# Tokens per expert counted once for all batches, and the last output columns stored in two halves

## The chip, the cores and the metric

The kernel runs on one core of a Trainium2 chip. The metric is the device time of one execution in microseconds (us), given as the median of the runs. TensorE (PE) does the matrix products, VectorE (DVE) and ScalarE (ACT) the elementwise work and the evictions from PSUM, GpSimd (POOL) some subtractions and the weight loads, and SyncE (SP) issues most of the other DMAs.

## The reference

Packed attention, and a mixture of experts behind it, for 8 batches of 576 tokens, 8 heads of 64:

```python
p_packed = sm_attn(p, k, v)                 # 32 packed rows for each head
out = sm_attn(q, p_packed, p_packed)        # back to 576 tokens
x = out.transpose(0, 2, 1, 3).reshape(4608, 512)
expert_idx = argmax(normalised(x) @ normalised(expert_emb).T / tau)
out[mask_e] = gate_w * (relu(x[mask_e] @ w1[e]) @ w2[e])   # e: the token's expert, of 8
```

## The kernel before

Each batch is tiled into five blocks of up to 128 tokens (`NC5`), and its feed-forward part runs with one expert, guessed early by `guess`. `route` computes the router's logits of all tokens and `oh`, a one-hot row of the chosen expert for each token; `counts` adds up `oh` over the tokens with two TensorE products against a column of ones, and `gates_main` multiplies the counts by `sel`, the one-hot row of the guessed expert, into `rest_f`. At the end of the program five VectorE operations turn `rest_f` into `rest_i`, the tokens that the guess did not cover; every engine loads their sum into a register and branches on it. A general path inside that branch does the uncovered batches anew; with these inputs it is passed over.

The order of work is written out by hand inside `tc.manual_schedule()`: engines run their instructions in the order in which the Python generators emit them. `ffn(b)` is the main stream. For each batch it emits `hidden` (the product with w1, 16 pieces f of 6 products each, line 932, evicted by ScalarE at 934 and VectorE at 935), then the columns of the last 320 tokens (line 960), then two blocks of 128 tokens, c = 0 and c = 1 (line 978). After each few products it yields, and the loop over `work` emits a step of the next batch's attention, `att_main(b + 1)`, with `route` at its end. While c = 1 runs, `ffn` also emits `w1_rows` of the next batch (line 850; the rows that go through w1). For the first batch the interleaving follows the string table `PLAN`.

`route` works in two groups of token blocks. For each block and half m, VectorE reduces the logits (line 704), and ScalarE squares the rows into a scratch tile `scr` only for their sum (line 708: an ACTIVATE and a read of the accumulator). `scr` has two buffers, taken in turn. PSUM tiles with the tag `pf` have four buffers, shared by `hidden`, the stored blocks and `counts`.

`store_main` gives the functions that store. A block is evicted by ScalarE (line 1254) and goes out as four DMAs of 32 token rows of 512 columns, 64 KB each (line 1264). In the last batch, block c = 1 is computed in two halves of 256 columns; both are evicted separately, and the four DMAs are issued after the second one, two by SyncE and two by ScalarE.

Of the kernel before, what the change touches and what calls it, by code (L numbers as in the profile page):

```python
# [17 lines left out]
P = 128  # L18
# [5 lines left out]
def kernel(  # L24
# [55 lines left out]
    for e in range(E):  # L80
        nc.vector.memset(ecol[:, e : e + 1], float(e))
    rest_f = cp.tile([1, B], F32, name="rest_f")
    rest_i = cp.tile([1, B + 1], I32, name="rest_i")

    def rsqrt(x, y, tag, eng=nc.vector):
# [66 lines left out]
    class Batch:  # L152
        def __init__(self):
            for name in ("kT", "qT", "s1", "mx", "p1", "sums", "rinv", "pp2", "s2", "p1T"):
                setattr(self, name, {})
            self.begun = self.soft = False

    def load_nat(b, n):

# [364 lines left out]
    def guess(x, late=0, engine=mybir.EngineType.Pool, total=None):  # L524
        pt = ps.tile([P, 512], F32, name="pu", tag="pf")
        if total is not None:

            for n in range(NPR):
                nc.tensor.matmul(
                    pt[:1, :E], total[:, n : n + 1], enT[:, n], start=(n == 0), stop=(n == NPR - 1)  # L530
                )
        else:
            for g in range(NG):
                nc.tensor.matmul(pt[:1, :E], itau, x.ppf[:, g, D:], start=(g == 0), stop=(g == NG - 1))
        yield
        m8 = sm.tile([1, 8], F32, name="m8", tag="m8")
        idx = sm.tile([1, 8], U32, name="idx", tag="idx")
        nc.vector.max(m8, pt[:1, :E])
        nc.vector.max_index(idx, m8, pt[:1, :E])
        gi = sm.tile([1, 1], F32, name="gi", tag="gi")  # L540
        nc.vector.tensor_copy(gi, idx[:, 0:1])
        x.sel = sm.tile([1, E], F32, name="sel", tag="sel")
        nc.vector.tensor_scalar(
            out=x.sel, in0=ecol[:1], scalar1=gi, scalar2=None, op0=ALU.is_equal
        )
        yield from idle(late)
        x.e = nc.values_load(idx[0:1, 0:1], engines=[engine], min_val=0, max_val=E - 1)
# [133 lines left out]
    def route(x, fine=False):  # L681
        lgs, sss = x.routed
        for c0, c1 in ((0, 2), (2, NC5)):
            pts = [pb.tile([P, 1024], F32, name="pt", tag="pb") for _ in range(2)]
            for c in range(c0, c1):
                for g in range(NG):
                    for n in range(2 * c, min(2 * c + 2, S // 64)):
                        for h in range(HB):
                            at = 512 * (h % 2) + 256 * g + XW * (c - c0)
                            nc.tensor.matmul(  # L690
                                pts[h // 2][64 * (n % 2) : 64 * (n % 2) + 64, at : at + XW],
                                x.at[32 * h : 32 * h + 32, g, 64 * n : 64 * n + 64],
                                x.ppf[32 * h : 32 * h + 32, g],
                                start=True,
                                stop=True,
                                tile_position=(32 * h, 64 * (n % 2)),
                            )
            yield
            views = [pt.rearrange("p (b s) -> p b s", s=256) for pt in pts]
            for c in range(c0, c1):  # L700
                r = rows(c)
                for m in range(2):
                    v = views[m][:r, :, XW * (c - c0) : XW * (c - c0) + XW]
                    nc.vector.tensor_reduce(  # L704
                        lgs[:r, m, c], v[:, :, D:].rearrange("p b e -> p e b"), axis=AX.X, op=ALU.add
                    )
                    scr = sb.tile([P, 4, D], F32, name="scr", tag="scr", bufs=2)
                    nc.scalar.activation(  # L708
                        scr[:r], v[:, :, :D], AF.Square, accum_out=sss[:r, m, c : c + 1]
                    )  # L710
                yield

        lg = sm.tile([P, NC5, E], F32, name="lgt", tag="lgt")
        ss = sm.tile([P, NC5], F32, name="sst", tag="sst")
        nc.vector.tensor_tensor(out=lg, in0=lgs[:, 0], in1=lgs[:, 1], op=ALU.add)
        nc.gpsimd.tensor_tensor(out=ss, in0=sss[:, 0], in1=sss[:, 1], op=ALU.add)
        x.lg, x.ss = lg, ss
        if fine:
            yield
        nc.vector.tensor_scalar_mul(lg, lg, itau)  # L720
        mx = sm.tile([P, NC5, 1], F32, name="lmx", tag="lmx")
        nc.vector.tensor_reduce(mx, lg, axis=AX.X, op=ALU.max)
        nc.vector.tensor_tensor(
            out=lg, in0=lg, in1=mx.broadcast_to([P, NC5, E]), op=ALU.subtract
        )
        oh = sm.tile([P, NC5, E], F32, name="oh", tag="oh")
        nc.vector.scalar_tensor_tensor(
            out=oh, in0=lg, scalar=0.0, in1=code.broadcast_to([P, NC5, E]),
            op0=ALU.is_ge, op1=ALU.mult,
        )  # L730
        nc.vector.tensor_reduce(mx, oh, axis=AX.X, op=ALU.max)
        nc.vector.tensor_tensor(
            out=oh, in0=code.broadcast_to([P, NC5, E]), in1=mx.broadcast_to([P, NC5, E]),
            op=ALU.is_equal,
        )
        x.oh = oh

    def counts(x):
        oh = x.oh
        pt = ps.tile([P, 512], F32, name="pu", tag="pf")  # L740
        nc.tensor.matmul(
            pt[:1, : 4 * E], ones, oh[:, 0:4].rearrange("p c e -> p (c e)"), start=True, stop=True
        )
        nc.tensor.matmul(pt[:1, 4 * E : 5 * E], ones[:64], oh[:64, 4], start=True, stop=True)
        cnt = sm.tile([1, E], F32, name="cnt", tag="cnt")
        nc.vector.tensor_reduce(
            cnt, pt[:1, : 5 * E].rearrange("p (c e) -> p e c", c=NC5), axis=AX.X, op=ALU.add
        )
        x.cnt = cnt


    def gates(x, eng=nc.vector):
# [115 lines left out]
                yield  # L868


    def ffn(x, store, late=False, after=None, end=False):
        if late:
            x.G = sb.tile([P, 2, NG, F], F32R, name="G", tag="G")
            x.g32, x.gs = [], 0
# [96 lines left out]
        for c in range(NCT):  # L971

            w = 256 if end and c == NCT - 1 else 512
            for at in range(0, 512, w):
                pf = ps.tile([P, 512], F32, name="pf", tag="pf")
                for f in range(NF):
# [17 lines left out]
                    if c == NCT - 1 and hasattr(after, "w1g"):  # L994
                        next(after.w1g, None)
                        next(after.w1g, None)
                    elif c == NCT - 1 and hasattr(after, "lg"):
                        after.w1g = w1_rows(after)
                        next(after.w1g)
                last.append((c, pf, at, w))  # L1000
# [2 lines left out]
            store(*t)  # L1003
        if hasattr(after, "w1g"):
            drain(after.w1g)

    STF = 5

# [9 lines left out]


    bat = [Batch() for _ in range(B)]  # L1020
    NAT = 2 * NPR + NG
    seq = [(b, i) for b in range(1, B) for i in range(NAT)]
    seq[NPR : 2 * NPR + NG] = [(1, i) for i in (8, 9, 4, 5, 6, 7)]
# [20 lines left out]
    def att_main(b):  # L1044
# [2 lines left out]
            prefetch(5)  # L1047
            yield from keys(x, nat_main(1), pns[1])
        if b:
            if b > 1:  # L1050
                counts(bat[b - 1])
            yield from att1(x, nat_main(b), b == 1)
            if b == 1:
                expert = guess(x)
                next(expert)
                query_scores(x)
                yield
            if b > 1:
                expert = guess(x)
                next(expert)  # L1060
# [18 lines left out]
            route_tiles(x)  # L1079
        yield from second  # L1080
        x.soft = True
        if b == B - 1:
            yield from idle(2)
            counts(x)

    def begin():

# [152 lines left out]
    def gates_main(b):  # L1240
        x = bat[b]
        yield from gates(x, nc.vector if b else nc.gpsimd)
        hit = sm.tile([1, E], F32, name="hit", tag="hit")
        nc.vector.tensor_tensor(out=hit, in0=x.cnt, in1=x.sel, op=ALU.mult)
        nc.vector.tensor_reduce(rest_f[:, b : b + 1], hit, axis=AX.X, op=ALU.add)

    def store_main(b):
        x = bat[b]

        def store(c, pf, at, w):  # L1250
# [5 lines left out]
                pf[:, :w].rearrange("p (t q j) -> p t q j", q=HB, j=32),  # L1256
                AF.Copy, scale=x.gate[:, c : c + 1],
            )
            if at + w < DM:
                return  # L1260
            for a in range(HB):
                n = HB * c + a
                queue = nc.scalar if at and a % 2 else nc.sync
                queue.dma_start(out_tokens(b)[:, n if b else 2 * n], o[32 * a : 32 * a + 32])

        tails = []

# [51 lines left out]
    def route_first():  # L1319
        route_tiles(bat[0])  # L1320
        yield from route(bat[0], True)
        yield
        counts(bat[0])

    with tc.manual_schedule():
        begun = begin()
# [39 lines left out]
        run(PLAN[0])  # L1366
        for b in range(B):
            after = bat[b + 1] if b + 1 < B else None
            work = ffn(bat[b], store_main(b), late=b == 0, after=after, end=b == B - 1)
            for n, _ in enumerate(work):  # L1370
                if b == 0:
                    run(PLAN[n + 1] if n + 1 < len(PLAN) else "srag")
# [9 lines left out]
                    next(gate, None)  # L1382


    nc.vector.tensor_scalar(
        out=rest_f, in0=rest_f, scalar1=-1.0, scalar2=float(S), op0=ALU.mult, op1=ALU.add
    )
    nc.vector.tensor_copy(rest_i[:, 0:B], rest_f)
    tot = sm.tile([1, 1], F32, name="tot")
    nc.vector.tensor_reduce(tot, rest_f, axis=AX.X, op=ALU.add)  # L1390
    nc.vector.tensor_copy(rest_i[:, B : B + 1], tot)
    n_rest = nc.values_load(rest_i[0:1, B : B + 1], min_val=0, max_val=B * S)
    with tc.If(n_rest > 0):
        with tc.For_i(0, B, 1) as b:
# [101 lines left out]
```

## Time and profile before

| | |
|---|---|
| median of 3 runs | 428.49 us (428.44 to 429.5) |
| time of the profiled execution | 429.1 us |
| its span, first to last instruction | 427.4 us |
| TensorE busy | 414.4 us, 97% |
| VectorE, ScalarE, GpSimd busy | 309.0, 217.4, 141.4 us |
| granted TensorE clock, mean | 0.997 |

The busy time of an engine is the union of its instructions. Sequencer work (semaphore waits, branches, DMA issues) is not counted as busy; in timelines it is marked by a q behind the engine's name.

### The profile page before, as it was taken

The page shows a single profiled execution, that of the slowest core. Times are in us where ns is not written, and L with a number is a line of the kernel's source. Part 1 is how long each engine was busy: PE and PEld are TensorE (multiplying, and loading weights), DVE is VectorE, ACT ScalarE, POOL GpSimd, SP SyncE. Part 2 cuts the span into 40 slices and gives each one's busy share as a digit, 9 for nine tenths or more (in the row PEclk, how much of TensorE's full clock was granted, in tenths as well). Part 3 has the DMA queues.
Part 4 walks back from the last instruction along what each step waited for, and adds up shares of the span by engine and source line. Part 5 has one row for each costly group of instructions (what it writes and reads, how often), then busy time and mean ns, then how long its engine had stood idle before and what let it go on. Part 6 is the DMA issues. An engine that isn't in the chain of part 4 may idle for free.

```text
span 427.4 us, 12605 instructions
## 1 busy us (share of the span) xinstructions
PE 414.4 (97%) x4802; PEld 348.3 (81%) x4803; DVE 309.0 (72%) x978; ACT 217.4 (51%) x652; POOL 141.4 (33%) x188
## 2 busy tenths in 40 slices
PE   7889999999999999999999999999999999999994
PEld 6536878589986989789886989869896899869983
DVE  5567768878986889758978689768997689646320
ACT  2446634784436734476426843466534744456300
POOL 1428845362404503053402604054222524045000
PEclk9999999999999999999999999999999999999998
DMA  7989989895999789964999379983899604640032
GB/s 221 278 271 295 257 226 274 248 217 140 270 313 247 200 220 333 280 173 124 265 363 217 103 222 309 297 196 106 226 347 246 154 2 163 233 88 26 1 64 54
DMA packets 48020, 88.36 MB, mean 207 GB/s; under 512 B 11016, under 2 KB 29512, under 8 KB 47952
## 3 DMA queue, kind: packets, MB, share of 16 engines
q1 hardware_dynamic: 39456, 57.83, 51.0%
q0 software_dynamic: 7968, 29.43, 20.5%
q8 instruction: 40, 0.66, 0.7%
q10 hardware_dynamic: 528, 0.21, 0.2%
q14 instruction: 28, 0.23, 0.2%
HBM read 78.00 MB, written 9.44 MB: 205 GB/s over the span
## 4 chain that ended last, share of the span: by engine, by line
PE 85%; DMA 8%; DVE 2%; ACT 1%; issue 0%; SPq 0%; ACTq 0%; DVEq 0%
PE pf L960 25%; PE pf L932 21%; PE pf L978 21%; DMA nat<-in_q 4%; PE pt L690 4%; PE pt L259 3%; PE pt L850 3%; PE pt L386 2%; DMA nat<-in_v 2%; PE pt L366 2%; DMA itau<-in_moe_tau 1%; DMA w1t<-in_moe_w 1%; PE pf L911 1%; ACT scr L708 1%; PE pf L892 1%; PE pt L892 1%
## 5 line engine op out<-in xcount | busy, mean ns | idle before, releaser
L826 POOL TENSOR_TENSOR w2s<-w2r,w2s 128x512 fp32r<-128x512 f32 x64 | 81.8, 1287 | 124.4 <-ACT w2s L825 123.0
L960 PE MATMUL pf<-hT,w2s 128*128 128x320 f32 x768 | 120.7, 312 | 0.0
L960 PEld LDWEIGHTS pf<-hT,w2s 128*128 128x128 f32 x768 | 113.0, 188 | 4.3 <-issue 3.3
L932 PE MATMUL pf<-AT,G 128*128 128x288 f32 x720 | 103.8, 298 | 0.1
L932 PEld LDWEIGHTS pf<-AT,G 128*128 128x128 f32 x720 | 97.3, 188 | 4.8 <-ACT hT L934 2.3
L978 PE MATMUL pf<-w2s,hT 128*128 128x512 f32 (+1 forms) x408 | 95.1, 385 | 0.0
L978 PEld LDWEIGHTS pf<-w2s,hT 128*128 128x128 f32 x408 | 71.9, 188 | 20.6 <-issue 5.9
L935 DVE SCALAR_TENSOR_TENSOR hT<-pf,hT 128x288 fp32r<-128x288 f32 x128 | 56.3, 446 | 23.9 <-ACT hT L934 23.9
L934 ACT ACTIVATE hT<-pf 128x288 fp32r<-128x288 f32 x128 | 51.3, 414 | 35.2 <-PE pf L932 34.4
L708 ACT ACTIVATE scr<-pt 128x256 f32<-128x256 f32 (+1 forms) x80 | 29.7, 378 | 40.0 <-DVE lg L704 40.0
L825 ACT CAST w2s<-w2r 128x512 fp32r<-128x512 f32 x64 | 38.7, 624 | 3.4 <-issue 3.4
L801 POOL DMA_DIRECT2D w1t<-in_moe_w x14 | 10.7, 766 | 78.6 <-DVE st L590 74.0
L864 DVE TENSOR_TENSOR G<-pt,G 128x512 fp32r<-128x512 f32 x28 | 18.7, 688 | 13.6 <-ACT G L863 13.6
L787 ACT COPY gt<-gate 32x2 f32<-32x2 f32 (+1 forms) x128 | 24.6, 192 | 6.5 <-DVE gate L772 4.2
L1271 DVE STREAM_TRANSPOSE ot<-pf 128x320 f32<-128x320 f32 x32 | 16.0, 499 | 13.3 <-PE pf L960 11.2
L863 ACT CAST G<-pt 128x512 fp32r<-128x512 f32 x28 | 15.7, 588 | 15.7 <-DVE G L864 12.1
L611 ACT CAST AT<-at 128x576 fp32r<-128x576 f32 x16 | 10.8, 673 | 25.3 <-DVE at L608 25.3
L593 ACT ACTIVATE st<-st 128x576 f32<-128x576 f32 (+1 forms) x17 | 11.2, 658 | 21.9 <-issue 19.9
L704 DVE TENSOR_REDUCE lg<-pt 128x8 f32<-128x32 f32 (+1 forms) x80 | 11.5, 174 | 14.8 <-PE pt L690 9.9
L289 DVE STREAM_TRANSPOSE kt<-nat 128x576 f32<-128x576 f32 x28 | 21.2, 762 | 0.1
L1254 ACT ACTIVATE o<-pf,gate 128x512 f32<-128x512 f32 (+1 forms) x17 | 11.4, 668 | 18.8 <-issue 14.3
L809 POOL DMA_DIRECT2D w2r<-in_moe_w x28 | 19.8, 712 | 0.0
(179 smaller groups left out, 491.9 us busy)
## 6 DMA issues: line engine op xcount, KB each, us to landing
nat<-in_k SPq DMA_DIRECT2D x112, 140.0 KB, 3.3
nat<-in_q SPq DMA_DIRECT2D x112, 140.0 KB, 4.7
w1t<-in_moe_w POOLq DMA_DIRECT2D x14, 1024.0 KB, 9.6
w2r<-in_moe_w POOLq DMA_DIRECT2D x28, 512.0 KB, 12.4
nat<-in_v SPq DMA_DIRECT2D x32, 160.0 KB, 4.6
out<-ot SPq DMA_DIRECT2D x28, 160.0 KB, 3.7
nat<-in_v SPq DMA_DIRECT2D x32, 128.0 KB, 4.4
out<-o SPq DMA_DIRECT2D x62, 64.0 KB, 1.7
```

What stands on the lines that cost most here:

```text
L289: nc.vector.transpose(kt.rearrange("p (n i) -> p n i", i=32), t)
L708: nc.scalar.activation(scr[:r], v[:, :, :D], AF.Square, accum_out=sss[:r, m, c : c + 1])
L787: copy(dst[32 * a : 32 * a + 32, k : k + HB * (n - 1) + 1 : HB], src[32 * k : 32 * k + 32, NCT : NCT + n],)
L809: queue.dma_start(t, w2e[:, 2 * i : 2 * i + 2, :])
L825: nc.scalar.copy(hi, raw)
L826: eng.tensor_tensor(out=lo, in0=raw, in1=hi.bitcast(F32), op=ALU.subtract)
L864: nc.vector.tensor_tensor(out=x.G[:, 1, g, fs], in0=src, in1=x.G[:, 0, g, fs].bitcast(F32), op=ALU.subtract,)
L932: nc.tensor.matmul(pf[:, :HS], w, r, start=(n == 0), stop=(n == len(ops) - 1))
L934: nc.scalar.activation(hT[:, 0, f, cs], pf[:, :HS], AF.Relu)
L935: nc.vector.scalar_tensor_tensor(out=hT[:, 1, f, cs], in0=pf[:, :HS], scalar=0.0, in1=hT[:, 0, f, cs].bitcast(F32), op0=ALU.max, op1=ALU.s ...
L960: nc.tensor.matmul(pf[:, : S - TL], x.w2s[f][:, m, mt * P : mt * P + P], hT[:, a, f, TL:], start=(n == 0), stop=(n == len(ops) - 1),)
L978: nc.tensor.matmul(pf[:, :w], hT[:, a, f, c * P : (c + 1) * P], x.w2s[f][:, m, at : at + w], start=(f == 0 and i == 0), stop=(f == NF - 1 ...
```

## The change

The eight calls of `counts` in the main path go, with their two VectorE operations each in `gates_main` and the five at the end. All one-hot rows lie in one tile `hot`, all guesses in one tile `guessed`, and a new generator `count_all` counts all batches with two wider products. It is advanced inside `ffn` of batch 6: its products come ahead of `w1_rows` of batch 7, its VectorE steps follow one by one. To hold `hot`, `scr` has one buffer instead of two. The last block of the last batch is stored half by half: four DMAs of 32 KB by SyncE after the first half (each token row in four pieces of 64 columns, 256 bytes), four by ScalarE after the second.

```diff
+    hot = cp.tile([P, B, NC5, E], F32, name="hot")
+    guessed = cp.tile([1, B, E], F32, name="guessed")
...
-                    scr = sb.tile([P, 4, D], F32, name="scr", tag="scr", bufs=2)
+                    scr = sb.tile([P, 4, D], F32, name="scr", tag="scr")
...
-        oh = sm.tile([P, NC5, E], F32, name="oh", tag="oh")
+        oh = x.oh if x.oh is not None else sm.tile([P, NC5, E], F32, name="oh", tag="oh")
...
+    def count_all():
+        pt = ps.tile([P, 512], F32, name="pu", tag="pf")
+        nc.tensor.matmul(
+            pt[:1, : B * 4 * E], ones, hot[:, :, 0:4].rearrange("p b c e -> p b (c e)"),
+            start=True, stop=True,
+        )
+        at = B * 4 * E
+        nc.tensor.matmul(
+            pt[:1, at : at + B * E], ones[:64], hot[:64, :, 4], start=True, stop=True
+        )
+        yield
+        cnt = sb.tile([1, B, E], F32, name="cnts", tag="scr")
+        nc.vector.tensor_reduce(
+            cnt, pt[:1, :at].rearrange("p (b c e) -> p b e c", b=B, c=4), axis=AX.X, op=ALU.add
+        )
+        yield
...
+        nc.vector.tensor_copy(rest_i[:, 0:B], rest_f)
...
                     if c == NCT - 1 and hasattr(after, "w1g"):
                         next(after.w1g, None)
                         next(after.w1g, None)
+                        next(more, None)
                     elif c == NCT - 1 and hasattr(after, "lg"):
+                        next(more, None)
                         after.w1g = w1_rows(after)
                         next(after.w1g)
...
         if b:
-            if b > 1:
-                counts(bat[b - 1])
             yield from att1(x, nat_main(b), b == 1)
...
-        if b == B - 1:
-            yield from idle(2)
-            counts(x)
...
         yield from gates(x, nc.vector if b else nc.gpsimd)
-        hit = sm.tile([1, E], F32, name="hit", tag="hit")
-        nc.vector.tensor_tensor(out=hit, in0=x.cnt, in1=x.sel, op=ALU.mult)
-        nc.vector.tensor_reduce(rest_f[:, b : b + 1], hit, axis=AX.X, op=ALU.add)
...
-            if at + w < DM:
+            if w < DM:
+                part = lambda t: t.rearrange("p (q n) -> p q n", q=HB)[:, :, at // HB : (at + w) // HB]
+                for a in range(HB):
+                    queue = nc.scalar if at else nc.sync
+                    queue.dma_start(
+                        part(out_tokens(b)[:, HB * c + a]), part(o[32 * a : 32 * a + 32])
+                    )
                 return
...
         yield from route(bat[0], True)
-        yield
-        counts(bat[0])
...
+            more = count_all() if b == B - 2 else iter(())
+            work = ffn(bat[b], store_main(b), late=b == 0, after=after, end=b == B - 1, more=more)
```

## Rows read from the trace of the kernel before

**Rows 1.** The head of the page: span, and busy time of each engine.
```profile
span 427.4 us, 12605 instructions
PE 414.4 (97%) x4802; PEld 348.3 (81%) x4803; DVE 309.0 (72%) x978; ACT 217.4 (51%) x652; POOL 141.4 (33%) x188
```

**Rows 2.** Timeline of TensorE in batch 2 (start, duration, engine, line, operation, count).
```profile
136.47 0.95 PE L932 MATMUL pf<-AT,G 128*128 128x288 f32 x6
137.35 0.22 PE L741 MATMUL pu<-oh,ones 128*1 128x32 f32 x2
...
137.51 0.43 PE L259 MATMUL pt<-kt,pw 64*32 64x288 f32 x2
```

**Rows 3.** Timeline around the count of the last batch.
```profile
370.38 4.45 PE L978 MATMUL pf<-w2s,hT 128*128 128x512 f32 x18
...
374.02 0.20 DVE L732 TENSOR_TENSOR oh<-code,lmx 128x40 f32<-128x40 f32 x1
...
374.76 0.22 PE L741 MATMUL pu<-oh,ones 128*1 128x32 f32 x2
...
375.03 0.96 PE L978 MATMUL pf<-w2s,hT 128*128 128x512 f32 x3
...
377.73 0.69 DVE L864 TENSOR_TENSOR G<-pt,G 128x512 fp32r<-128x512 f32 x1 [1.68 <-ACT G L863]
```

**Rows 4.** Timeline of TensorE at the first batch's full-precision products.
```profile
26.25 2.21 PE L911 MATMUL pf<-at,g 128*128 128x288 f32 x8
```

**Rows 5.** Timeline of the squares of the last batch, second group.
```profile
370.68 0.39 ACT L708 ACTIVATE scr<-pt 128x256 f32<-128x256 f32 x1 [2.49 <-DVE lg L704]
370.96 0.20 ACT L708 ACTIVATION_READ_ACCUMULATOR scr<-pt 128x1 f32 x1
371.05 0.38 ACT L708 ACTIVATE scr<-pt 128x256 f32<-128x256 f32 x1
371.19 0.19 DVE L704 TENSOR_REDUCE lg<-pt 128x8 f32<-128x32 f32 x1 [0.51 <-ACT scr L708]
```

**Rows 6.** Timeline of VectorE's logit reductions of batches 0 and 1.
```profile
54.44 0.19 DVE L704 TENSOR_REDUCE lg<-pt 128x8 f32<-128x32 f32 x1 [0.17 <-ACT scr L708]
...
78.03 0.18 DVE L704 TENSOR_REDUCE lg<-pt 64x8 f32<-64x32 f32 x1 [0.18 <-ACT scr L708]
```

**Rows 7.** Timeline of batch 1's start.
```profile
83.93 0.67 DVE L864 TENSOR_TENSOR G<-pt,G 128x512 fp32r<-128x512 f32 x1
...
89.47 5.79 PE L932 MATMUL pf<-AT,G 128*128 128x288 f32 x42
...
90.22 0.46 DVE L935 SCALAR_TENSOR_TENSOR hT<-pf,hT 128x288 fp32r<-128x288 f32 x1 [0.87 <-ACT hT L934]
...
93.59 0.45 DVE L935 SCALAR_TENSOR_TENSOR hT<-pf,hT 128x288 fp32r<-128x288 f32 x1
```

**Rows 8.** Timeline of the end: evictions and store issues.
```profile
416.14 6.21 SPq L1264 DMA_DIRECT2D out<-o  x6
418.27 0.47 ACT L1254 ACTIVATE o<-pf,gate 128x256 f32<-128x256 f32 x1 [2.15 <-PE pf L978]
...
421.57 0.85 ACTq L1264 DMA_DIRECT2D out<-o  x2
```

**Rows 9.** Instructions of the branch (L1393) and the program's end (L1492): durations, first and last start.
```profile
L1393 SPq EVENT_SEMAPHORE  x9: 17/17/17, 425.1 to 425.7; - x9
...
L1393 SPq COMPARE_BRANCH  x1: 53/53/53, 422.4 to 422.4; - x1
...
L1492 SPq EVENT_SEMAPHORE  x14: 17/28/28, 425.8 to 427.4; - x14
```

**Rows 10.** DMA issues: count, KB each, median us from issue to landing.
```profile
out<-o SPq DMA_DIRECT2D x62, 64.0 KB, 1.7
...
pn<-in_p SPq DMA_DIRECT2D x24, 16.0 KB, 2.4
out<-o ACTq DMA_DIRECT2D x2, 64.0 KB, 2.0
```

More of the change, by code (lines that the diff above doesn't have):

```diff
@@ L156, in __init__ @@
             self.begun = self.soft = False
+            self.oh = self.sel = None
     def load_nat(b, n):
@@ L541, in guess @@
         nc.vector.tensor_copy(gi, idx[:, 0:1])
-        x.sel = sm.tile([1, E], F32, name="sel", tag="sel")
         nc.vector.tensor_scalar(
@@ L749, in counts @@
         x.cnt = cnt
+    def count_all():
[14 more added lines that the diff above has]
+        yield
+        nc.vector.tensor_tensor(
+            out=cnt, in0=cnt, in1=pt[:1, at : at + B * E].rearrange("p (b e) -> p b e", b=B),
+            op=ALU.add,
+        )
+        yield
+        nc.vector.tensor_tensor(out=cnt, in0=cnt, in1=guessed, op=ALU.mult)
+        yield
+        nc.vector.tensor_reduce(rest_f.unsqueeze(2), cnt, axis=AX.X, op=ALU.add)
+        yield
+        nc.vector.tensor_scalar(
+            out=rest_f, in0=rest_f, scalar1=-1.0, scalar2=float(S), op0=ALU.mult, op1=ALU.add
+        )
+        yield
+        nc.vector.tensor_copy(rest_i[:, 0:B], rest_f)
+        tot = sm.tile([1, 1], F32, name="tot")
+        nc.vector.tensor_reduce(tot, rest_f, axis=AX.X, op=ALU.add)
+        yield
+        nc.vector.tensor_copy(rest_i[:, B : B + 1], tot)
     def gates(x, eng=nc.vector):
@@ L868, in w1_rows, with ffn @@
                 yield
-    def ffn(x, store, late=False, after=None, end=False):
+    def ffn(x, store, late=False, after=None, end=False, more=iter(())):
         if late:
@@ L1005, in ffn @@
             drain(after.w1g)
+        drain(more)
     STF = 5
@@ L1020 @@
     bat = [Batch() for _ in range(B)]
+    for b, x in enumerate(bat):
+        x.oh, x.sel = hot[:, b], guessed[:, b]
     NAT = 2 * NPR + NG
@@ L1262, in store @@
                 n = HB * c + a
-                queue = nc.scalar if at and a % 2 else nc.sync
-                queue.dma_start(out_tokens(b)[:, n if b else 2 * n], o[32 * a : 32 * a + 32])
+                nc.sync.dma_start(out_tokens(b)[:, n if b else 2 * n], o[32 * a : 32 * a + 32])
         tails = []
@@ L1368 @@
             after = bat[b + 1] if b + 1 < B else None
-            work = ffn(bat[b], store_main(b), late=b == 0, after=after, end=b == B - 1)
+            more = count_all() if b == B - 2 else iter(())
+            work = ffn(bat[b], store_main(b), late=b == 0, after=after, end=b == B - 1, more=more)
             for n, _ in enumerate(work):
@@ L1382 @@
                     next(gate, None)
[L1385 to L1391, printed above, removed]
     n_rest = nc.values_load(rest_i[0:1, B : B + 1], min_val=0, max_val=B * S)
```

1 line of the change is left out of this document (added).

## The prediction

> **What bounds the kernel.** I read the head of the page first: TensorE is busy 97% of the span [rows 1], so an instruction taken off it counts, and any other edit counts only where it makes TensorE wait or stands behind its last product. Then the timelines of TensorE around each count, to price what goes. From about 105 us on, products follow each other there at one steady pace, and the gaps are changes between kinds of product; the reader is to see that in [rows 2] nothing waits. Then ScalarE and VectorE in the start-up stretch, up to about 95 us, because there two engines besides TensorE run with hardly a pause. Last the stretch from 416 us, where the products end and something else sets the end.
>
> **Counts that go.** In batches 2 to 7 a count stands ahead of the key scores: its first product starts at 137.35, the scores at 137.51 [rows 2]. The change of product kind ahead of it stays, so 0.16 goes each time; six such places, 0.96. The last batch's count stands inside the stored blocks [rows 3]: 18 products in 4.45 us are 0.24 each with the tail of the last taken off, the next would start at 374.67, and starts at 375.03, and its three take 0.96 where 0.87 is their pace: 0.45. Batch 0's count lies alike, 0.45. Together 1.86.
>
> **The count that comes.** Full-precision products of 288 columns go at 2.21 us for eight, 0.26 to 0.28 each [rows 4]; two of 256 columns and two of 64 make 0.6. What is fixed in a count is 0.2: 0.27 from its first product to the next block in [rows 3], less some 0.07 for its few columns. It then stands beside `w1_rows`, whose change of kind is paid already. Between 0.5 (nothing fixed) and 1.0 (with a change back), I take 0.75. It needs batch 7's one-hot rows, ready at 374.22, and is emitted after the first three products of c = 1, at about 375.9: 1.7 us of cover [rows 3]. Its eight VectorE steps on one partition fall where VectorE waits 1.68 for ScalarE [rows 3]: nothing, and without that cover two small steps, under 1 us, ahead of the last of batch 7's G, which has to be there only when the w1 products begin. The two VectorE operations removed per batch stood beside TensorE work: nothing.
>
> **One buffer for the squares.** This is the part that can cost. With two buffers a square starts 0.37 after the one before, 370.68 and 371.05, while that one's accumulator is read until 371.16 [rows 5]. With one it has to wait for this read; a reduction of VectorE that waits for such a read starts 0.03 after it, at 371.19 [rows 5]. So squares would follow at 0.52 instead of 0.37: 0.15 for each wait. From below, nothing: if ScalarE's own order were taken as enough, the squares would still overlap. I take 0.15, since a tile given out anew waits for its last user here whatever the engine.
>
> In batches 2 to 7 squares come in pairs with VectorE work between, and all is far ahead of TensorE's need: nothing. In the last batch the six squares of the second group end about 0.75 later and VectorE's chain to the one-hot rows moves by 3 times 0.15, inside the 1.7 of cover above. In batches 0 and 1 the reductions run in step with the squares: each reduction waits for the square of the block before [rows 6], and VectorE, which has no idle time of its own there, carries the delay on. A first group puts one such wait ahead of its last reduction; a second group three, in batch 0 two (another ScalarE operation lies between). That is 1 + 2 + 1 + 3 = 7 waits, 1.05 us by 78.03, the last reduction of the four groups. VectorE's queue behind it is batch 0's gate, batch 1's router, the transposes of batch 2's keys, and then G of batch 1 at 83.93 [rows 7]. One count removed ahead of that gives back 0.05. So G, the evictions of the w1 products behind it on ScalarE, and VectorE's second half of them (90.22, waiting for ScalarE) come 1.0 late.
>
> Does TensorE feel it? The 42 products from 89.47 are pieces f1 to f7; the last six start at about 94.25. Piece f7 needs the PSUM buffer of f3, four allocations back, and VectorE leaves f3 at 93.59 + 0.45 = 94.04 [rows 7]. Cover 0.2. So f7 is held until 1.0 - 0.2 = 0.8 after its old place. And this pins TensorE there: the 0.61 that the first two counts give back before that point are lost in the same wait. What counts on TensorE is then +0.8 for the wait, -0.8 for the five counts of batches 3 to 7's starts, -0.45 and +0.75 for the last count and its replacement: +0.3.
>
> **The end.** SyncE's last two issues end at 416.14 + 6.21 = 422.35 [rows 8]; its branch is at 422.4, its next instruction only at 425.1, then nine and fourteen waits, and the span closes at 427.4 [rows 9]. ScalarE's last store, started at 422.0, lands 2.0 later [rows 10], ahead of all that: the end is SyncE's issue time plus 5.0. After the change SyncE issues its four from 418.74 [rows 8] to about 420.5, and by itself would end at 425.5. ScalarE now issues four in a row from 421.57, 0.43 each [rows 8]; the fourth starts at 422.9 and by 2.0 lands at 424.9. SyncE meets that landing inside its nine waits, of which some 0.3 may be left, and from the fourteen on 1.6 are needed: 426.9 to 427.0, a gain of 0.45. Bounds: 0.9 (landing after 1.7, no wait left) and a loss of 0.3 (landing after 2.7).
>
> The price of the landing is bounded by loads of 16 KB in pieces of 128 bytes, 2.4, against 1.7 for stores of 64 KB in pieces of 2 KB [rows 10]; the half stores, 32 KB in 256 bytes, lie between, and I keep 2.0, ScalarE's own row. The Trainium skill (DMA: Bandwidth & Descriptors, Specifications) states that transfers under 512 bytes are done as read-modify-write and fall below line rate. That speaks against pieces of 256 bytes; no store of such pieces is in this trace.
>
> **Sum.** +0.3 on TensorE and -0.45 at the end are -0.15 on the profiled 427.4, or 429.1 to 428.95. On the median, 428.49, that is 428.3.
>
> **Rivals.** *The squares' waits don't reach TensorE.* For it: only one place, f7, is pinned, with a cover of 0.2 that a different pace of VectorE would widen; against it: no idle time in the chain. If VectorE's chain stays where it was, f7 still holds TensorE after 0.2 of gain: -0.2 - 0.8 - 0.45 + 0.75 - 0.45 = -1.15, 427.3; with everything given back, -1.86 + 0.75 - 0.45 = -1.56, 426.9. Chance 0.22.
>
> *All twenty squares of batches 0 and 1 are paid in full*: ScalarE, not VectorE, carries the delay on, and the gate copies, G casts and evictions behind the squares start later by 20 times 0.15 = 3.0. Then f7 waits 2.8, and the sum is 2.8 - 0.8 + 0.3 - 0.45 = +1.85, 430.3. It decides from a delay of some 2.5 at f7. Against it: the reductions wait for earlier squares, and ScalarE waits for VectorE behind them. Chance 0.12.
>
> *The halves land late.* The last landing 0.7 later, by the two rows of landing above, gives 425.6, and the end 0.25 behind that of before instead of 0.45 ahead: 429.0. The rule on 512 bytes would act here. Chance 0.08.
>
> **Numbers.** The forecast, 428.3, has 0.58. About 0.3% (1.3 us) is what a measurement of this kernel can tell from no change. The first rival lies half beyond that, and a shorter chain in the forecast gives some more: faster 0.20. Slower is the second rival, 0.12; the rest, 0.68, is no change. Range: from the first rival's 426.9 to 429.5, which is the third rival with a chain 0.5 longer.
>
> **What would show it.** Squares 0.5 apart in all batches; the reduction of 78.03 about a microsecond later; TensorE waiting for VectorE at the first batch's f6 or f7, near 94; key scores right behind the w1 products; ScalarE's four issues as the last of all, and SyncE's branch near 420.5. It is wrong if the squares still overlap, if the waits at 94 don't come, or if SyncE's long pause after its branch moves to ScalarE.

## The result and the profile after

The changed kernel takes 431.38 us (median of 7 runs, 430.54 to 432.11), the kernel before 428.56 beside it on the same chip (428.44 to 430.09): ratio 1.0062, 95% interval 1.0049 to 1.0075 (the ratio is taken from all the runs and is not the quotient of the two medians). It is 2.8 us slower, where 428.3 was forecast and the range ended at 429.5.

The head of the page of the profiled execution after (its own time is 432.11):

```profile
span 430.4 us, 12590 instructions
PE 414.6 (96%) x4774; PEld 349.0 (81%) x4775; DVE 303.6 (71%) x958; ACT 223.3 (52%) x652; POOL 142.1 (33%) x188
```

Beside [rows 1] TensorE issues 28 instructions fewer and VectorE 20 fewer, and the span is 3.0 longer. TensorE's last product ends at 421.55 for 421.03, so 0.5 of the 3.0 arises ahead of it. The other 2.5 lie behind the last product, where the kernel now needs 8.9 us for 6.4.

**The end after.** Timeline of SyncE's and of ScalarE's queue from 416 us (L1303 stores whole columns, L1297 halves), then the half stores by line (durations in ns: least, median, most), SyncE's waits from 415 us (us in total, times, longest), and SyncE's instructions of the branch and of the program's end:

```profile
416.67 1.74 SPq L1303 DMA_DIRECT2D out<-o  x4
419.29 6.29 SPq L1297 DMA_DIRECT2D out<-o  x4
```

```profile
418.79 0.47 ACT L1288 ACTIVATE o<-pf,gate 128x256 f32<-128x256 f32 x1 [2.15 <-DMA out<-o]
421.59 0.47 ACT L1288 ACTIVATE o<-pf,gate 128x256 f32<-128x256 f32 x1 [2.32 <-PE pf L1015]
422.10 1.82 ACTq L1297 DMA_DIRECT2D out<-o  x4
```

```profile
L1297 SPq DMA_DIRECT2D out<-o x4: 315/380/1567, 419.3 to 424.0; - x4
L1297 ACTq DMA_DIRECT2D out<-o x4: 371/443/445, 422.1 to 423.5; - x4
...
DMA to landing us min/median/max: 1.5/3.1/3.4
```

```profile
SPq L1297 <- DMA out<-o: 3.5, 1, 3.5
SPq L1424 <- SPq L1424: 2.4, 1, 2.4
```

```profile
L1424 SPq EVENT_SEMAPHORE  x9: 17/17/17, 428.1 to 428.7; - x9
...
L1424 SPq COMPARE_BRANCH  x1: 53/53/53, 425.6 to 425.6; - x1
```

The data of SyncE's four half stores are there from 419.27 on, yet issuing them takes 6.29 us. In the middle stands one wait of 3.5 us, and what it waits for is a store. The instructions say which: SyncE issues two at 419.29 and 419.67, the third at 423.65. Eight semaphores count these stores in turn, and each issue first waits for what its semaphore has counted so far. The third store counts its completion on semaphore 108, as the first of ScalarE's half stores does, which lands at 423.64. So SyncE waits for the other queue's store of the second half before it goes on with the first. The semaphores are fixed when the program is built; why ScalarE's store, which the Python code emits later, comes first on 108 is not shown here. The fourth issue then takes 1.57 for the usual 0.43. SyncE branches at 425.64 for 422.41 [rows 9], its first wait behind the branch comes at 428.12 for 425.11, and the span closes 4.8 after the branch, as it did 5.0 after it before.

**Batch 7's start after.** Timeline of VectorE, GpSimd and TensorE's weight loads from 381 us (L765 to L786 are the count, L972 is VectorE's part of hT, L863 GpSimd's part of w2):

```profile
381.92 0.20 DVE L769 TENSOR_TENSOR cnts<-cnts,pu 1x64 f32<-1x64 f32 x1
382.16 1.09 DVE L774 TENSOR_TENSOR cnts<-cnts,guessed 1x64 f32<-1x64 f32 x1
383.28 0.21 DVE L776 TENSOR_REDUCE rest_f<-cnts 1x8 f32<-1x64 f32 x1
383.53 0.93 DVE L778 TENSOR_SCALAR rest_f<-rest_f 1x8 f32<-1x8 f32 x1
384.49 1.22 DVE L782 CAST rest_i<-rest_f 1x8 int32<-1x8 f32 x1
385.63 0.14 DVE L784 TENSOR_REDUCE tot<-rest_f 1x1 f32<-1x8 f32 x1
385.81 0.14 DVE L786 CAST rest_i<-tot 1x1 int32<-1x1 f32 x1
385.88 1.53 DVE L972 SCALAR_TENSOR_TENSOR hT<-pf,hT 128x288 fp32r<-128x288 f32 x4
```

```profile
381.88 5.04 POOL L863 TENSOR_TENSOR w2s<-w2r,w2s 128x512 fp32r<-128x512 f32 x4 [4.47 <-ACT w2s L862]
```

```profile
386.37 0.82 PEld L969 LDWEIGHTS pf<-AT,G 128*128 128x128 f32 x6 [0.55 <-DVE hT L972]
```

Three operations on 8 or 64 numbers take about a microsecond each, and hT, which is behind them in VectorE's queue, starts at 385.88. TensorE waits 0.55 for it. GpSimd's four subtractions (the expectations call them additions) end at 383.17, 384.43, 385.69 and 386.92, and the three slow ones of VectorE end 0.08, 0.03 and 0.02 after the first three of these ends.

**The start-up after.** Squares of the second group of batch 1, VectorE's last reduction, and TensorE's weight loads of piece f7:

```profile
76.79 0.39 ACT L710 ACTIVATE scr<-pt 128x256 f32<-128x256 f32 x1 [0.33 <-DVE lg L706]
77.07 0.19 ACT L710 ACTIVATION_READ_ACCUMULATOR scr<-pt 128x1 f32 x1
77.30 0.39 ACT L710 ACTIVATE scr<-pt 128x256 f32<-128x256 f32 x1
```

```profile
78.82 0.18 DVE L706 TENSOR_REDUCE lg<-pt 64x8 f32<-64x32 f32 x1 [0.32 <-ACT scr L710]
```

```profile
94.78 0.82 PEld L969 LDWEIGHTS pf<-AT,G 128*128 128x128 f32 x6 [0.17 <-DVE hT L972]
```

The squares stand 0.51 apart, the last reduction [rows 6] has moved from 78.03 to 78.82, and TensorE waits at f7. The same product of TensorE, before and after, is 0.57 later at 95 us, then gains 0.14 to 0.18 at each batch's start where a count is gone, and stands 0.07 ahead at 377.7, the new count included. Batch 7's start loses 0.6, and it ends 0.52 late. Batch 2's start and the new count on TensorE (in [rows 2] the key scores start 1.04 after the w1 products, here 0.88):

```profile
137.02 0.95 PE L969 MATMUL pf<-AT,G 128*128 128x288 f32 x6
137.90 0.47 PE L262 MATMUL pt<-kt,pw 64*32 64x288 f32 x8
```

```profile
375.29 0.59 PE L755 MATMUL pu<-hot,ones 128*1 128x256 f32 x2
```

The 0.57 at 95 us is not to be put down to the change as it stands. Five kernels of the experiments (`halves`, `halves22`, `all_act`, `one_three`, `three_queues`) have the program of before up to 416 us, and in their profiles the same product stands at 95 us between 0.74 ahead of the kernel before and 0.34 behind it. The start-up differs that much from one execution to the next. From 95 us to 416 us four of the five keep their place within 0.06, and the fifth moves by 0.4, so the steps behind 95 us can be read from one pair of profiles, and the offset at 95 us cannot.

### The profile page after: what moved, and what is told of

Read it like the earlier page. It is cut to its first block, busy times and chain, and to the rows that moved or that the text cites. A ratio compares the mean times of both kernels' runs of the same rounds, so it can differ in the third digit from the quotient of the medians.

```text
span 430.4 us, 12590 instructions
## 1 busy us (share of the span) xinstructions
PE 414.6 (96%) x4774; PEld 349.0 (81%) x4775; DVE 303.6 (71%) x958; ACT 223.3 (52%) x652; POOL 142.1 (33%) x188
## 4 chain that ended last, share of the span: by engine, by line
PE 85%; DMA 6%; DVE 3%; ACT 2%; issue 1%; SPq 1%; DVEq 0%; ACTq 0%
PE pf L997 25%; PE pf L969 21%; PE pf L1015 20%; PE pt L692 4%; PE pt L262 4%; PE pt L887 3%; PE pt L389 2%; DMA w1t<-in_moe_w 2%; DMA nat<-in_q 2%; DMA nat<-in_v 2%; PE pt L369 2%; PE pf L1148 1%; ACT scr L710 1%; PE pt L240 1%; DVE G L901 1%
## 5 line engine op out<-in xcount | busy, mean ns | idle before, releaser
L863 POOL TENSOR_TENSOR w2s<-w2r,w2s 128x512 fp32r<-128x512 f32 x64 | 81.9, 1290 | 123.7 <-ACT w2s L862 120.0
L972 DVE SCALAR_TENSOR_TENSOR hT<-pf,hT 128x288 fp32r<-128x288 f32 x128 | 56.0, 445 | 26.3 <-ACT hT L971 26.3
L710 ACT ACTIVATE scr<-pt 128x256 f32<-128x256 f32 (+1 forms) x80 | 30.7, 384 | 40.4 <-DVE lg L706 38.2
```

Of the source, the lines that this page charges most:

```text
L710: nc.scalar.activation(scr[:r], v[:, :, :D], AF.Square, accum_out=sss[:r, m, c : c + 1])
L863: eng.tensor_tensor(out=lo, in0=raw, in1=hi.bitcast(F32), op=ALU.subtract)
L972: nc.vector.scalar_tensor_tensor(out=hT[:, 1, f, cs], in0=pf[:, :HS], scalar=0.0, in1=hT[:, 0, f, cs].bitcast(F32), op0=ALU.max, op1=ALU.s ...
```

## The experiments

Each ratio is to the kernel before, timed beside it on the same chip, with its 95% interval.

**The stores alone**: the kernel before with the change's store, and nothing else of it (`halves`).

```
-            if at + w < DM:
+            if w < DM:
...
+                for a in range(HB):
+                    queue = nc.scalar if at else nc.sync
+                    queue.dma_start(
+                        part(out_tokens(b)[:, HB * c + a]), part(o[32 * a : 32 * a + 32])
+                    )
                 return
...
-                queue = nc.scalar if at and a % 2 else nc.sync
-                queue.dma_start(out_tokens(b)[:, n if b else 2 * n], o[32 * a : 32 * a + 32])
+                nc.sync.dma_start(out_tokens(b)[:, n if b else 2 * n], o[32 * a : 32 * a + 32])
```

> The kernel before with only the store in halves. Theory A (shared completion semaphore: SyncE's third store of the first half is queued behind ScalarE's first of the second half): SyncE's third store starts about 1.5 us after ScalarE's first one, SyncE's branch comes near 425, and the time is 2 to 3 us above that of before, 430.5 to 431.5. Theory B (pieces of 256 bytes fill SyncE's queue): the same time. Both: TensorE's products as before.

Measured: 430.28 for 428.84, ratio 1.0035 (1.0023 to 1.0047). SyncE's waits from 415 us:

```profile
SPq L1263 <- DMA out<-o: 3.4, 1, 3.4
```

The wait is there without the counts: SyncE's third store goes out at 423.50, ScalarE's first on semaphore 108 landed at 423.49. The loss is 1.0 to 2.0 us by the interval, at or below the lower end of the 2 to 3 that were expected. More than half of the change's loss is the store.

**The counts alone**: the changed kernel with the store of before (`counts`).

> The changed kernel with the store of before. Both theories: the end of the program as before (SyncE's last issue plus 5.0), TensorE 0.5 late at the last batch's columns, 0.6 of it from the VectorE steps of the count; the time 0.3 to 0.7 above that of before, 429.0.

Measured: 429.47, ratio 1.0021 (1.0010 to 1.0033). Of the two parts, 0.35% and 0.21%, neither gains, and their sum is near the 0.62% of the whole. TensorE loses 0.6 at batch 7's start here too; the end is that of before. That TensorE would be 0.5 late at the end missed: this profile came out of the start-up 0.4 ahead of the kernel before at 95 us, and ends 0.5 ahead.

**One queue for both halves**: the changed kernel, with the second half's four stores on SyncE as well (`one_queue`).

```
-                    queue = nc.scalar if at else nc.sync
+                    queue = nc.sync
```

> The changed kernel, with the second half's four stores issued by SyncE as well. Theory A: SyncE's third store follows the second within 0.5 us, since no store of another engine lies between them; the last of eight is issued near 423.8, and the time is some 1.5 us under that of the changed kernel, about 430. Theory B: the third store is held again by the pieces ahead of it until about 423, the second half waits behind it, and the time is that of the changed kernel or above, 431.4 to 433.

Measured: 430.49, ratio 1.0042 (1.0029 to 1.0055). SyncE issues the first half at 418.32, 418.69, 419.17 and 419.64, with no wait: the hold belongs to the semaphore shared between two queues, not to four half stores in a row. It now has eight to issue, branches at 423.38 and closes the span 5.0 later. By the ratios it is 0.2%, 0.9 us, faster than the changed kernel, where 1.5 was expected. The first store landed in 1.5 us, the next two in 3.9 and 3.7, of which the next experiment shows the cause.

**All of the last stores on ScalarE**: the kernel before, whole columns, no half stores (`all_act`).

```
-                queue = nc.scalar if at and a % 2 else nc.sync
+                queue = nc.scalar if at else nc.sync
```

> The kernel before, with all four stores of the last block, whole rows, issued by ScalarE. If SyncE's last issue sets the end: SyncE branches near 418.8, the end is that of ScalarE's last landing (some 425) plus 2, and the time is 0.3 to 0.6 under that of before, 428.0. If it does not: no change, or 0.8 later by ScalarE's two further issues, 429.3.

Measured: 429.96, ratio 1.0016 (1.0003 to 1.0029): a loss, where a gain was expected if SyncE's last issue set the end. SyncE's instructions of the branch:

```profile
L1393 SPq EVENT_SEMAPHORE  x9: 17/17/17, 421.3 to 427.0; - x9
...
L1393 SPq COMPARE_BRANCH  x1: 53/53/53, 418.8 to 418.8; - x1
```

SyncE branches 3.6 earlier and then stands in its waits, until 426.47, for ScalarE's third store: issued at 422.52, landed at 426.45, 3.9 after its issue. So whole columns, in pieces of 2 KB, land late as well. The DMA queues of this kernel from 423.7 to 425.4, from 424.4 to 425.38 and from 425.4 to 426.2 (packets, MB, share of 16 engines):

```profile
q10 hardware_dynamic: 63, 0.07, 15.8%
q8 instruction: 1, 0.02, 6.3%
```

```profile
q14 instruction: 1, 0.01, 3.4%
```

```profile
q10 hardware_dynamic: 6, 0.01, 6.0%
```

q10 carries ScalarE's stores. Most of their packets are through at 424.39. Then none starts for a microsecond, and the last six follow from 425.41 on. What lies between is one packet of q8: 16 KB of instructions, from 423.71 to 425.44. The same is seen in the profiles of the other kernels whose stores have pieces left over: in the changed kernel the 16 KB packets end at 421.84 and 425.19 and left-over pieces of stores start at 421.84 and 425.18; with the halves alone 422.19 and 425.94, and 422.17 and 425.91; with one queue 421.40 and 424.81, and 421.39 and 424.80 (this is what the two stores of 3.9 and 3.7 waited for). What is left over is 9 of the 144 packets of a half store, one part in sixteen, which fits the share of one of the 16 DMA engines, busy with the instructions; the record of a packet does not name its engine. In the kernel before, the second 16 KB run from 423.80 to 425.22, and its last store packet ends at 423.59: it slips through by 0.2. The Trainium skill (Runtime: NRT & Kernel Launch, Instruction fetch mechanics) states that instructions are refilled in blocks of 16 KiB by DMA; the size agrees. What such a load does to a store beside it is shown by these rows alone.

**The second half split over both queues**, first half on SyncE, on the kernel before (`halves22`). Beside the stores alone:

```
-                    queue = nc.scalar if at else nc.sync
+                    queue = nc.scalar if at and a % 2 else nc.sync
```

> Before with the last columns' two halves stored one after the other, the first by SyncE, the second by both queues in turn as before splits them. Theory (what made halves late is that some pieces queue on the one DMA engine that at 423.8 us loads 16 KB of instructions for 1.3 us, and that the third store of SyncE was held by a semaphore): the second half is issued by 422.4 and its last packets start before 423.8, so that the last landing is 424.0 to 424.3 and the time that of before, ratio 0.9995 to 1.0007, unless SyncE is held again, which would give 1.003. Rival (pieces of 256 bytes land late in themselves, 3 us for 1.7): the last landing at 425 or later with SyncE not held, ratio 1.002 or more.

Measured: 430.52, ratio 1.0039 (1.0025 to 1.0053). The hold came back, so the landing could not be tested here. SyncE's waits:

```profile
SPq L1263 <- DMA out<-o: 2.6, 1, 2.6
```

SyncE's first store of the second half is on semaphore 108 and waits until 423.15; ScalarE's, also on 108, landed at 423.13. The first half's stores stood free and landed in 1.5, 3.4, 3.2 and 2.9, with a 16 KB packet from 420.35 to 421.52 between them. Pieces of 256 bytes are not slow in themselves: the one that met no load of instructions landed in 1.5.

**One store on SyncE, three on ScalarE**, whole columns, on the kernel before (`one_three`), and **one on SyncE, two on ScalarE, one on GpSimd** (`three_queues`).

```
-                queue = nc.scalar if at and a % 2 else nc.sync
+                queue = nc.scalar if at and a else nc.sync
...
-                queue = nc.scalar if at and a % 2 else nc.sync
+                queue = (nc.sync, nc.scalar, nc.gpsimd, nc.scalar)[a] if at else nc.sync
```

> Before with the last block's four whole stores shared otherwise: one by SyncE, three by ScalarE. Theory for the end: the span closes 5.0 us after SyncE's last issue, and not before a landing plus 2.2 us; of a store some pieces wait on the one DMA engine that loads 16 KB of instructions from about 423.7 to 425.2 us. SyncE's branch would come at 421.95 for 422.4 and allow an end 0.46 us earlier, but ScalarE's third store is issued at about 422.45, its pieces are on the way until 423.9, and those on that engine land at 425.7 to 426.5: the span closes at 427.9 to 428.7, 0.5 to 1.3 us later than before's, ratio 1.001 to 1.003. Rival (stores land about 2 us after their issue, and what was late in the halves came from their 256-byte pieces): third landing at 424.5, 0.4 us faster, ratio 0.999.

Measured: 429.19 for 428.53, ratio 1.0006 (0.9994 to 1.0018): the time tells neither theory apart. The profiled execution does. SyncE's instructions of the branch:

```profile
L1393 SPq EVENT_SEMAPHORE  x9: 17/17/17, 425.0 to 426.7; - x9
...
L1393 SPq COMPARE_BRANCH  x1: 53/53/53, 422.2 to 422.2; - x1
```

ScalarE's third store goes out at 422.76 and lands at 426.27, 3.5 later; its last pieces start at 425.05, and the 16 KB packet ends at 425.09. SyncE's branch was early, its waits were not over before that landing.

> Before with the last block's four whole stores on three queues: one by SyncE, two by ScalarE as before, one by GpSimd. Theory (the end is SyncE's last issue plus 5.0): SyncE's branch at 421.95, ScalarE's landings as before at 423.5 and 424.05; if GpSimd's store lands by 424.9 the span closes 0.4 us earlier, ratio 0.9985 to 0.9995. If GpSimd issues so slowly that its pieces meet the load of instructions at 423.7, its landing at 425.7 or later gives 1.001 to 1.003. Rival (the end hangs on something else than SyncE): no change from before, ratio 1.000.

Measured: 429.16, ratio 1.0023 (1.0005 to 1.0041): a loss, though GpSimd's store landed at 424.59, before the 424.9 that the theory asks for. SyncE's branch came 0.4 after the last eviction for 0.9 before, and all stores had landed by 424.8 (two of them 3.5 after their issue, with no piece left over behind the 16 KB packet of 423.08 to 424.08; why stays open). A third thing set the end, which no theory had named. GpSimd's drains at the program's end, in the changed kernel (L1523), where GpSimd stores nothing, and with this store (L1492):

```profile
L1523 POOLq DRAIN  x3: 50/107/3823, 392.3 to 430.1; - x3
```

```profile
L1492 POOLq DRAIN  x3: 46/107/4438, 422.1 to 427.1; - x3
```

The longest drain takes 3.8 us there too, but begins at 392.3, when GpSimd has done its work and nobody waits. Behind a store issued at 421.1 it lasts from 422.13 to 426.57, 2.0 beyond the landing of that store (424.59), and every engine waits for it.

**One scratch tile for the squares**, alone, on the kernel before (`scr1`).

```
-                    scr = sb.tile([P, 4, D], F32, name="scr", tag="scr", bufs=2)
+                    scr = sb.tile([P, 4, D], F32, name="scr", tag="scr")
```

> Before with one scratch tile for the squares and nothing else. Theory (each square waits for the accumulator read of the one before it, 0.51 us apart for 0.37, and the lateness stays in TensorE's order, 0.57 us at 95 us in the profile of the change): 0.4 to 0.8 us slower, ratio 1.001 to 1.002, offset of TensorE +0.5 to +0.8 from 95 us on. Rival (the first batch's slack takes it): ratio 0.9995 to 1.0005.

Measured: 429.18 for 428.75, ratio 1.0016 (1.0004 to 1.0028): the time is as the theory has it. The offset is not, 0.24 behind the kernel before at 95.1 us for 0.5 to 0.8, and it could not show the tile either: TensorE loses 0.56 between 57 and 95 us here, and 0.4 to 0.7 in four of the five kernels with two tiles and the program of before. What does tell one tile from two are two pauses. TensorE's weight loads with one tile, then with two (`halves`):

```profile
55.22 0.14 PEld L534 LDWEIGHTS pu<-ppf,itau 128*1 128x1 f32 x4 [0.97 <-ACT ppf L435]
...
68.79 0.90 PEld L690 LDWEIGHTS pt<-ppf,at 32*64 32x64 f32 x64 [0.57 <-issue]
```

```profile
54.90 0.14 PEld L534 LDWEIGHTS pu<-ppf,itau 128*1 128x1 f32 x4 [0.55 <-ACT ppf L435]
...
68.47 0.90 PEld L690 LDWEIGHTS pt<-ppf,at 32*64 32x64 f32 x64 [0.30 <-issue]
```

The squares are 0.51 apart, and TensorE waits 0.42 longer for ScalarE at 55 us, of which 0.14 is left behind its next wait; the pause at 69 us is 0.27 longer. The first pause is 0.97 in all five profiles with one tile and 0.55 in all nine with two, the second 0.57 to 0.59 and 0.30 to 0.32. So one tile costs TensorE 0.41 by 69 us. At f7 nothing waits in this profile.

**Five of the count's steps later**: the counts alone, but the multiplication by the guess and what follows it are issued in the token tail of batch 7, one after each four products (`late`).

```
                 if n % 4 == 3:
+                    if end and mt:
+                        next(more, None)
                     yield
...
+            if b == B - 2:
+                count = count_all()
+                more = (next(count) for _ in range(3))
+            else:
+                more = count if b == B - 1 else iter(())
```

> The counts alone (new count, one scratch tile, the stores of before), but only the count's products, its first sum and its addition stay where the change puts them; the multiplication by the guess, the sum, the difference, the two casts and the total are issued one by one in the token tail of batch 7, between groups of four matmuls. Theory (the five late steps, 0.2 to 1.2 us each beside GpSimd's four additions of 1.3 us, hold VectorE's share of hT and cost TensorE 0.6 us at 386 us): the wait at 386 us is gone, TensorE stands 0.6 us earlier at 395 us than in the counts alone, and the time is 428.6 to 429.1 beside 428.8 of before, ratio 0.9995 to 1.0005. Rival (TensorE waits there for ScalarE or for the weights as well, and VectorE was only last): the wait stays at 0.3 us or more and the time stays at a ratio of 1.002.

Measured: 428.78 for 428.75, ratio 1.0003 (0.9988 to 1.0017). Timeline of VectorE from 397 us, and of TensorE's weight loads from 381 us:

```profile
397.30 0.17 DVE L774 TENSOR_TENSOR cnts<-cnts,guessed 1x64 f32<-1x64 f32 x1
397.51 0.21 DVE L776 TENSOR_REDUCE rest_f<-cnts 1x8 f32<-1x64 f32 x1
...
399.19 0.12 DVE L778 TENSOR_SCALAR rest_f<-rest_f 1x8 f32<-1x8 f32 x1
399.34 0.16 DVE L782 CAST rest_i<-rest_f 1x8 int32<-1x8 f32 x1
```

```profile
382.08 5.03 PEld L969 LDWEIGHTS pf<-AT,G 128*128 128x128 f32 x37
```

The same operations take 0.17, 0.12 and 0.16 for 1.09, 0.93 and 1.22, and TensorE's wait is gone: 37 loads without a pause. GpSimd's last subtraction has ended at 391.1, ahead of all of them. TensorE is 0.49 ahead of the kernel before at 377 us and keeps it to the last product, which ends 0.48 earlier; in the counts alone it was 1.11 ahead at 377 us and 0.52 at 395. That it would stand 0.6 earlier at 395 us than in the counts alone missed, by the start-ups of the two profiles, which lie 0.6 apart at 95 us. The Trainium skill (SBUF — State Buffer, Who interferes with whom) states that VectorE and GpSimd share a pair of ports which one instruction holds for its whole length; that VectorE needs it for two inputs in SBUF and, with copies, casts and operations with a scalar, in its fast modes; and that reductions do not. The rows agree: L774 (both inputs in SBUF), L778 and L782 are slow beside GpSimd, while L769, which takes one input from PSUM, and the reductions L776 and L784 took 0.14 to 0.21 there. A cast does not wait each time, though: L786, of a single number, took 0.14 beside the fourth subtraction.

**Late steps, two scratch tiles**: the same, with two tiles in bfloat16 in the room of one (`late_scr2`), and, to tell the second tile from the smaller elements, **the kernel before with its two tiles in bfloat16** (`scr_bf16`). Nothing reads the tile; the sums stay in float32.

```
-                    scr = sb.tile([P, 4, D], F32, name="scr", tag="scr")
+                    scr = sb.tile([P, 4, D], mybir.dt.bfloat16, name="scr", tag="scr", bufs=2)
...
-        cnt = sb.tile([1, B, E], F32, name="cnts", tag="scr")
+        cnt = sb.tile([1, B, E], F32, name="cnts", tag="scr", bufs=2)
```

> As the late steps, and the squares' scratch back to two tiles, in bfloat16 so that two fit where one was (no one reads the tile itself, the sums leave in float32). Theory: with both faults of the counts gone only the gain of the seven counts is left. In the profile of the change that gain was 0.15 to 0.18 us for each count from batch 2 on, 0.76 in five, less 0.1 for the new count, so 427.9 to 428.4, ratio 0.998 to 0.999; the squares are 0.37 us apart again. Rival (squares in one scratch tile do not reach TensorE's order, the start-up of the profiles only differs by chance): the same time as the late steps alone.

> Before with its two scratch tiles in bfloat16, nothing else. It tells whether the gain of the late steps with two scratch tiles (ratio 0.997, beside 1.0003 with one tile in fp32) comes from the second tile or from the smaller elements. Theory (the second tile; the squares start 0.37 us apart and take 0.38 us at either size): the time of before, ratio 0.9993 to 1.0007. Rival (writing bfloat16 is itself worth something): ratio 0.999 or less.

Measured: with both, 427.61 for 428.75, ratio 0.9970 (0.9957 to 0.9983), faster than either kernel. The elements alone: 428.72 for 428.32, ratio 1.0011 (0.9996 to 1.0026), no gain. Squares of batch 1 with the late steps and two tiles:

```profile
76.67 0.38 ACT L710 ACTIVATE scr<-pt 128x256 bf16<-128x256 f32 x1 [0.32 <-DVE lg L706]
...
77.04 0.38 ACT L710 ACTIVATE scr<-pt 128x256 bf16<-128x256 f32 x1
```

A square takes 0.38 as before, and they start 0.37 apart again. Beside the late steps with one tile the second tile is worth 0.33% here, against the 0.16% that one tile costs by itself; the intervals overlap, and the difference stays open.

**The same with three queues at the end** (`best_three_queues`):

> The late steps with two scratch tiles in bfloat16, and the last block's four stores on three queues. If three queues give 0.4 us beside before, and the gain of the counts (ratio 0.997 in its own run) stays: 0.9955 to 0.9965, 426.8 to 427.2. If GpSimd's store lands late: 0.998 to 1.000.

Measured: 427.82 for 428.53, ratio 0.9987 (0.9975 to 0.9998). The 0.9955 to 0.9965 that was hoped for is missed: GpSimd's store takes back part of the gain, as it cost time by itself.

## Why the prediction was wrong

**The step that failed** is "SyncE issues its four from 418.74 [rows 8] to about 420.5". That the end is SyncE's issue time plus 5.0 held to 0.2: 4.8 to 5.0 from branch to end in the changed kernel, with the halves split over both queues and with one queue (5.7 with the halves alone, where the pause behind the branch was longer). But the four were priced by duration and data alone, and the third had to wait for a store of the other queue, because the two count on the same semaphore. That is 3.5 of waiting and 1.1 more for the fourth issue, and the branch came at 425.64. [rows 8] could not show it: in the kernel before, no issue of the last block waited for a landing. The halves alone show the loss without the counts, one queue shows four half stores without the wait.

**The landing** failed as well, hidden behind that. "The fourth starts at 422.9 and by 2.0 lands at 424.9": ScalarE's third and fourth landed at 426.37 and 426.57, 3.1 to 3.4 after their issue. The third rival had named late halves, with 0.7 and by the size of the pieces. What the runs show is a load of instructions, which holds one part in sixteen of a store and which whole columns meet too. With all stores on ScalarE the span closed 2.1 after the last landing. Had SyncE not been held, 426.57 plus that would have given, as an estimate, 428.6 to 428.7 for the span, still 1.2 behind that of before, of which 0.5 is TensorE's. So the store could not gain as it is, and the forecast's 0.45 of gain was lost twice over. The Trainium skill's rule on transfers under 512 bytes (DMA: Bandwidth & Descriptors, Specifications), quoted in the prediction, was not what made them late: ScalarE's half stores that met no load of instructions landed in 1.5 to 1.6, whole ones in 1.7 [rows 10].

**"Its eight VectorE steps on one partition fall where VectorE waits 1.68 for ScalarE: nothing"** was the second miss. Only the first falls there; the others come behind the last G and ahead of hT, beside GpSimd's subtractions, three of them at six to eight times their price alone. The bound of "under 1 us" held in size, 0.6 on TensorE, though it was meant for two small steps ahead of G. Moving the steps took the wait away.

**One scratch tile** behaved as forecast in its waits: 0.14 each for 0.15, the last reduction 0.79 later for 1.05. The way into TensorE's order was another. 0.41 is lost by 69 us, at two pauses for which the prediction has no term. At f7, where 0.8 was to be lost, TensorE waits 0.17 in the four one-tile profiles whose counts are gone, and not with the tile alone. That the changed kernel's +0.57 at 95 us lies near the +0.8 is in part luck, since the start-up alone moves that figure by as much. By itself the tile costs 0.16% of the time by the ratio, about 0.7 us, and 0.4 by the medians. The rival in which the squares don't reach TensorE is out by the pauses at 55 and 69 us, and so is the one of 3.0.

**The counts** went as forecast: 0.14 to 0.18 each for 0.16, 0.47 for the 0.45 of the last one, and about 0.55 for the 0.75 of the new one, inside its bounds. TensorE at 377.7 is 0.07 ahead, where the forecast's +0.3 would have it behind; 0.2 of the difference lies ahead of 95 us and 0.2 in the new count.

**The sum.** TensorE: +0.52 for +0.3, of which 0.6 is the VectorE steps; what lies ahead of 95 us is partly chance. The end: +2.5 for -0.45, of which SyncE's later branch, counted from the last product, is 2.7. Together 3.0 in the profile, 2.8 in the medians.

## What to carry to other kernels

A DMA issue can wait for a DMA of another queue with which it has nothing in common but the semaphore that counts both; before stores are spread over queues, look which issue is last on each semaphore, and whether an earlier one now stands behind it. At the end of a kernel, count each store twice: the issue, which delays the branch of the engine that issues it, and the landing, against the loads of instructions that run there; here stores whose packets were through before the 16 KB load landed in about 2 us, those with pieces left over behind it in 3 to 4. Small VectorE operations have no fixed price: look at what GpSimd does beside them, and put them where it rests; what was gained here came from the counts that went, once their replacement stood in an idle stretch and the squares kept their second tile. Before an offset of half a microsecond in one pair of profiles is put down to a change, look how far kernels that are the same up to that place lie apart.

## What the runs showed that was not expected

- From SyncE's branch to its next instruction 2.5 to 3.4 us pass (2.70 before, 2.48 after, 3.41 with the halves alone, 3.04 with the late steps). What sets this time stays open; 0.3 of the gain of the late steps was lost there in the profiled execution.
- An issue right behind a held one took 1.57 and 1.59 for 0.43. The hold is not needed for it: in the kernel before, SyncE's second store at 416.52 took 1.21, with a 16 KB load of instructions on the way from 416.33 to 417.36. In eight profiles an issue of SyncE lasts 0.92 to 1.42 beside such a load, and it ends 0.36 after the load does, as the two behind a hold end 0.39 after theirs; where no load runs at that place, as in the changed kernel, the same issue takes 0.42. No experiment moved the load.
- GpSimd's drain takes 3.8 us even where it has stored nothing for long, and 4.4 and 3.9 in the two kernels in which it stores last; there it came into the time.
- VectorE's operations on 8 numbers took 0.12 and 0.16 alone and 0.93 and 1.22 beside GpSimd's subtractions of 1.3.
